# A new order for the first unit of a fused attention and feed-forward kernel, with some scalings and low parts moved to GpSimd

## The chip, the cores and the metric

One core of a Trainium2 chip runs the whole kernel. The metric is device microseconds of one execution; the shown times are of three executions. TensorE multiplies matrices, VectorE and ScalarE work on tiles element by element (ScalarE also does the exponentials), GpSimd is the fourth compute engine, and SyncE issues loads. In the profile they are PE, DVE, ACT, POOL and SP.

## What is computed

Attention with 4 batches, 8 heads, 576 positions and head size 64, in two patterns: four heads see a plain band of 32 keys, four see every fourth key of the last 128. Then two feed-forward blocks on the 2304 tokens:

```python
attn = softmax(where(mask, q @ k.T / 8, -1e9)) @ v      # band of 32, or 32 keys in steps of 4
h = maximum(maximum(x @ w1, x @ w2), x @ w3)            # 512 -> 768
x = h @ w_out
h = x @ w_in                                            # 512 -> 2048
g = (a0 + a1*h + a2*h**2 + a3*h**3) / (1 + |b0|*|h| + |b1|*h**2 + 1e-6)
out = g @ w_out2
```

Weights arrive as float64; attention inputs and result are float32.

## The kernel before

**Two-part numbers.** Matrix products of the feed-forward blocks are made of three TensorE passes: a value is split into a high part (rounded by a ScalarE copy into the matmul's type) and a low part (the rest, by a subtraction), and high x high, high x low and low x high are summed (`mm3`). A float64 weight tile of 128x512 goes through five steps: `L` (load of the words, SyncE's queue, `cv_load` L521), `up` (`cv_up` L543, ScalarE), `bits` (`cv_bits` L552, VectorE, two operations), `hi` (`cv_hi` L560, ScalarE) and `lo` (`cv_lo` L573, VectorE: the subtraction of L579). `up` writes a buffer "cvt" that `lo` is the last to read; there are three of them (`CVT`, L156). The first unit converts 24 tiles so, 18 of the three input matrices and 6 of the output matrix.

**Units.** Tokens of the first block go in five units; the first has 384 tokens, two attention parts (0 and 1) of 192 positions. While the first unit's matmuls run, parts 2 and 3 of the attention are made for the next unit. Each part has a plain (p) and a dilated (d) half. All of the first unit is one list of words, `START` (L36), written out by hand: each word is issued in the list's order, and each engine takes its own instructions in that order (`manual_schedule`, L728). The words of a part: `S` scores and mask on TensorE (L302), `MX` maxima (VectorE), `D` subtraction (VectorE), `E` exponentials (ScalarE), `SM` sums, `SB` scaling by one over the sum (L406: two small VectorE operations, then a multiplication of the whole tile on VectorE, or with `act` one ScalarE copy per head and block), `X` transposes on TensorE (L417), `XC` copies of these out of PSUM, `V` the product with the values, `VH` and `VL` its high and low parts. `W:n` puts 4n multiplications of a dummy tile ahead of the next bank. Of the first block: `P:i` is the product with weight tile i (12 matmuls), `M:i` the maximum taken over the three matrices, `HH` and `HL` the parts of the result, `Y` the output columns (18 matmuls each), `YS` their copy out. A word in lower case with a digit is a load (`kp0`, `qd1`, `v0`). For c=3 the dilated scores have fewer keys than the tile's width, so `S3:d` also issues a fill of the rest on GpSimd:

```python
            if W < WD and not plain:
                nc.gpsimd.memset(sb[:, :, W:WD], 0.0)     # L350
```

The dilated tiles of parts 2 and 3 share one buffer. Behind the first unit come four more, then the second block, whose schedule is not touched.

Of the kernel before, what the change touches and what calls it, by code (L numbers as in the profile page):

```python
# [7 lines left out]
F32 = mybir.dt.float32  # L8
F32R = mybir.dt.float32r
AF = mybir.ActivationFunctionType  # L10
ALU = mybir.AluOpType
# [22 lines left out]


START = """  # L36
mk mkB T kp0 qp0 qd0 W:8 S0:p kd0 MX0:p kd1 E0:p W:4 S0:d,mm SM0:p MX0:d qd1 D0:d E0:d SB0:p S1:d
X0:p,1 L SM0:d MX1:d X0:p,0,pv up kp1 qp1 S1:p,mm SB0:d XC0:p,1 bits E1:d L up MX1:p D1:p
XC0:p,0 v0 X0:d,1,sc X0:d,0,pv XC0:d,0 XC0:d,1 W:2 V0:p,mm SB1:d V0:d,sc X1:d,1 bits qd2 v1 E1:p
X1:d,0,mm SM1:p hi lo L L qp2 SB1:p S2:d,pv XC1:d,1 X1:p,0 XC1:d,0 VH0:p VH0:d hi XC1:p,0 L  # L40
X1:p,1,mm VL0:p V1:d,mm L MX2:d up XC1:p,1 VL0:d V1:p,mm VH1:d bits VH1:p VL1:d S2:p VL1:p lo up hi
P:0 up MX2:p L P:1 E2:d lo bits P:2 hi M:0 k1 up bits L SB2:d M:1 lo bits P:3 L hi E2:p up M:2 lo L
bits L hi lo M:3 up HH:0 P:4 X2:d,1,mm bits hi qp3 up hi lo L X2:d,0,pv L SB2:p,act bits S3:p P:5 up
L M:4 lo XC2:d,1 L MX3:p P:6 X2:p,1 qd3 XC2:d,0 S3:d,pv L bits M:5 hi X2:p,0,mm up lo bits P:7 HL:0
up hi M:6 HH:1 lo bits MX3:d up hi XC2:p,0 lo hi L up bits lo M:7 E3:p P:8 P:9 hi bits lo M:8 up
P:12 L L hi bits E3:d lo hi SM3:d M:9 up lo HL:1 HH:2 up XC2:p,1 bits M:12 hi v2 bits L up hi
SB3:d,act P:10 lo M:10 up P:13 L bits P:11 M:13 L SM3:p P:14 V2:p,sc hi HL:2 V2:d,sc SB3:p,act M:11
lo X3:p,0 up lo bits L M:14 hi bits up X3:d,0,pv bits HH:4 XC3:p,0 L X3:d,1,mm hi X3:p,1,pv lo v3
HH:3 lo P:16 HL:4 hi XC3:d,1 lo up P:15 HL:3 up P:17 bits XC3:d,0 VH2:d M:15 bits up XC3:p,1 hi
VH2:p M:16 bits lo V3:p hi M:17 V3:d,tp lo VH3:p hi VH3:d lo HH:5 HL:5 Y:2 VL2:d VL3:d Y:0 YS:0 YS:2  # L50
Y:3 VL3:p YS:3 Y:1 VL2:p YS:1
"""

UNITS = {3: """
# [49 lines left out]
def kernel(  # L104
# [16 lines left out]
    nc = tc.nc  # L121
# [19 lines left out]
    M = CH // 4  # L141
# [147 lines left out]
    def attn_pieces(c):  # L289
# [116 lines left out]
        def SB(g, engine="dve"):  # L406
            sv, Q, W, U, sm = grp[g][:5]
            nc.vector.tensor_scalar_add(sm, sm, 1.0e-9)
            nc.vector.reciprocal(sm, sm)
            if engine == "dve":  # L410
                nc.vector.tensor_tensor(out=sv, in0=sv, in1=sm.to_broadcast([Q, U, W]),
                                        op=ALU.mult)
                return
            for n in range(U):
                nc.scalar.activation(out=sv[:, n], in_=sv[:, n], func=AF.Copy, scale=sm[:, n])
# [58 lines left out]
        def VL(g):  # L474
# [3 lines left out]
            if done_v[c] == 2 and c > 2:  # L478
                load_v(c + 1)

        return {"S": SC, "MX": MX, "D": DF, "E": E, "SM": SM, "SB": SB, "X": X, "XC": XC,
                "V": V, "VH": VH, "VL": VL}

    at_fn = {}

    def do(word):

        op, _, arg = word.partition(":")
        name, c = op.rstrip("0123456789"), int(op.lstrip("ABCDEFGHIJKLMNOPQRSTUVWXYZ"))
        if c not in at_fn:  # L490
            at_fn[c] = attn_pieces(c)
        at_fn[c][name](*[x if x.isalpha() else int(x) for x in arg.split(",")])
# [77 lines left out]
        cv[i][3] = slot  # L570
        nc.scalar.activation(out=slot[:, 0:512], in_=cv[i][2], func=AF.Copy)

    def cv_lo(i):  # L573
        kind, f, j = conv_seq[i]
        _, _, t, slot = cv.pop(i)
        if kind == "w2":
            nc.gpsimd.dma_start(out=w2d[f], in_=t)
        else:
            nc.vector.tensor_sub(slot[:, 512:1024], t, slot[:, 0:512].bitcast(F32))  # L579

    cv_at = {"load": 0, "up": 0, "bits": 0, "hi": 0, "lo": 0}
    cv_steps = (("hi", cv_hi, "bits"), ("lo", cv_lo, "bits"), ("up", cv_up, "load"),
                ("bits", cv_bits, "up"), ("load", cv_load, None))

    def w2_words(k):

        i = n_w1 + k
        cv_up(i)
        cv_bits(i)
        cv_lo(i)  # L590
        if k + RAW2 < 2 * F2:
            cv_load(i + RAW2)
# [11 lines left out]
    def m1_mm(u, f, j, cols=None):  # L604
        if (u, f, j) not in m1:
            m1[u, f, j] = bank("mm", "mm")[:, 0:SZ1[u]]
        cols = cols or slice(0, SZ1[u])
        x1h, x1l = x1[u]
        w = w1s[f, j]
        mm3(m1[u, f, j][:, cols], [(w[:, 128 * c:128 * c + 128], w[:, 512 + 128 * c:640 + 128 * c],  # L610
                                    x1h[:, c, cols], x1l[:, c, cols]) for c in range(KC)])

    def m1_max(u, f, j):
        o = m1[u, f, j]
        if j == 0:
            m1[u, f] = com.tile([128, T1], F32, tag="m", bufs=MB, name="m")[:, 0:SZ1[u]]
            nc.scalar.activation(out=m1[u, f], in_=o, func=AF.Copy)
        else:
            nc.vector.tensor_tensor(out=m1[u, f], in0=o, in1=m1[u, f], op=ALU.max)  # L619
# [75 lines left out]
    with ExitStack():  # L695
# [4 lines left out]
        mk = const.tile([128, 512], F32, name="mk")  # L700
# [17 lines left out]
        script = START.split()  # L718
        steps = {n: (fn, after) for n, fn, after in cv_steps}

        def cv_step(name):
            fn, after = steps[name]
            assert cv_at[name] < (cv_at[after] if after else n_w1)
            assert name != "lo" or cv_at["lo"] < cv_at["hi"]
            fn(cv_at[name])
            cv_at[name] += 1

        with tc.manual_schedule():  # L728
            for word in script:
                op, _, arg = word.partition(":")  # L730
                if op == "L":
                    cv_step("load")
                elif op in loads:
                    loads[op]()
                elif op == "W":
                    idle[0] = int(arg)
                elif op == "H":
                    m1_mm(0, 0, int(arg), slice(0, CH))
                elif op == "P":
                    f, j = divmod(int(arg), 3)  # L740
                    m1_mm(0, f, j, slice(CH if (0, f, j) in m1 else 0, 2 * CH))
                elif op == "M":
                    m1_max(0, *divmod(int(arg), 3))
                elif op in ("HH", "HL", "Y", "YS"):
                    {"HH": m1_hh, "HL": m1_hl, "Y": m1_y, "YS": m1_ys}[op](0, int(arg))
                elif op in steps:
                    cv_step(op)
                else:
                    do(word)

# [19 lines left out]
        for u in range(1, NU):  # L770
            last = u == NU - 1
            pieces = attn(u + 1) if not last else iter(())
            if last:
# [9 lines left out]
                with tc.high_priority(offset=-LATE_W2):  # L783
                    for _ in range(W2A):
                        load_w2(w2a)
                    for tag in ("x1h", "x1l"):
                        t = xa.tile([128, NP * T1], F32R, tag=tag, name="w2x")
                        load_w2(xa, t[:, 0:1024])
                        load_w2(xa, t[:, 1024:2048])
            slot = 0  # L790
# [132 lines left out]
        for g in range(NSL + 4):  # L923
            t, c = divmod(g, F2)
# [154 lines left out]
```

## Time and profile before

| | us |
|---|---|
| median of three executions (776.42 to 777.43) | 777.36 |
| the profiled execution | 777.2 |
| its span, first to last instruction | 775.4 |
| TensorE busy in the span | 767.7 |
| VectorE busy | 585.7 |
| ScalarE busy | 452.4 |
| GpSimd busy | 59.1 |

The profiled execution takes 1.8 us more than its span: what lies around the first and last instruction. It stands 0.16 us below the median. Busy times overlap, so they don't add up. GpSimd's busy time is nearly all the issuing of transfers. The first unit's list runs from the start of the span to about 86 us, where the last of its output columns is copied out.

### The profile page before, as it was taken

How to read it: one execution, taken by the hardware profiler on the slowest of the kernel's cores; microseconds unless marked ns; L12 is line 12 of the kernel's file. 1: busy time of each engine (PE TensorE's matmuls, PEld its weight loads, DVE VectorE, ACT ScalarE, POOL GpSimd, SP SyncE). 2: the span in 40 equal slices, each digit the busy share in tenths (PEclk: the TensorE clock that was granted, in tenths of full speed). 3: DMA queues.
4: the chain of work that ended last, by engine and by line, in shares of the span. 5: the costliest groups of instructions: out<-in, count | busy, mean ns of one | idle time of the engine just before them, and what ended most of it. 6: DMA issues, size and time to landing. Idle time of an engine off the chain costs nothing.

```text
span 775.4 us, 12062 instructions
## 1 busy us (share of the span) xinstructions
PE 767.7 (99%) x4656; PEld 661.1 (85%) x4656; DVE 585.7 (76%) x997; ACT 452.4 (58%) x841; POOL 59.1 (8%) x114
## 2 busy tenths in 40 slices
PE   8999999999999999999999999999999999999997
PEld 7999999988888888888888888888888888888996
DVE  5999477567635663465499998889888998888983
ACT  4997243333332333243597878677776768676872
POOL 0000222213121101000000001000000001000010
PEclk9999999999999999999999999999999999999999
DMA  9981577657556556632400011000110001000010
GB/s 342 401 347 49 173 227 240 192 167 232 194 168 182 163 184 219 204 109 88 143 0 1 1 55 55 1 1 3 66 42 1 1 27 55 1 0 1 1 55 27
DMA packets 28490, 85.67 MB, mean 110 GB/s; under 512 B 3664, under 2 KB 5456, under 8 KB 28432
## 3 DMA queue, kind: packets, MB, share of 16 engines
q1 hardware_dynamic: 19344, 52.17, 21.3%
q0 software_dynamic: 8800, 32.51, 11.4%
q8 instruction: 36, 0.59, 0.3%
q10 hardware_dynamic: 288, 0.22, 0.1%
q14 instruction: 22, 0.18, 0.1%
HBM read 67.06 MB, written 17.83 MB: 109 GB/s over the span
## 4 chain that ended last, share of the span: by engine, by line
PE 98%; ACT 1%; DVE 1%; issue 0%; ACTq 0%
PE mm L597 13%; PE mm L598 13%; PE mm L599 13%; PE h L597 8%; PE h L599 8%; PE h L598 8%; PE acc L909 8%; PE acc L911 8%; PE acc L910 8%; PE sc L341 3%; PE tpp L424 2%; PE pv L455 1%; PE pv L447 1%; PE sc L207 0%; ACT keys L397 0%; DVE mx L369 0%
## 5 line engine op out<-in xcount | busy, mean ns | idle before, releaser
L597 PE MATMUL mm<-x1h,w1s 128*128 128x512 f32 (+1 forms) x360 | 134.5, 374 | 0.0
L599 PE MATMUL mm<-x1h,w1s 128*128 128x512 f32 (+1 forms) x360 | 132.4, 368 | 0.0
L598 PE MATMUL mm<-x1l,w1s 128*128 128x512 f32 (+1 forms) x360 | 132.4, 368 | 0.0
L599 PE MATMUL h<-x2h,w2s 128*128 128x512 f32 (+1 forms) x280 | 103.0, 368 | 0.0
L598 PE MATMUL h<-x2l,w2s 128*128 128x512 f32 (+1 forms) x280 | 103.0, 368 | 0.0
L597 PE MATMUL h<-x2h,w2s 128*128 128x512 f32 (+1 forms) x280 | 103.0, 368 | 0.0
L909 PE MATMUL acc<-w2s,gh 128*128 128x512 f32 x252 | 98.1, 389 | 0.0
L910 PE MATMUL acc<-w2s,gh 128*128 128x512 f32 x252 | 98.1, 389 | 0.0
L911 PE MATMUL acc<-w2s,gl 128*128 128x512 f32 x252 | 96.2, 389 | 0.0
L857 ACT ACTIVATE q<-h 128x512 f32<-128x512 f32 x72 | 43.1, 598 | 85.4 <-PE h L599 84.1
L597 PEld LDWEIGHTS mm<-x1h,w1s 128*128 128x128 f32 x360 | 67.6, 188 | 9.1
L599 PEld LDWEIGHTS mm<-x1h,w1s 128*128 128x128 f32 x360 | 67.6, 188 | 8.6
L864 DVE SCALAR_TENSOR_TENSOR q<-q,cs,ab 128x512 f32<-128x512 f32 x72 | 54.0, 750 | 27.5 <-ACT ab L858 26.6
L598 PEld LDWEIGHTS mm<-x1l,w1s 128*128 128x128 f32 x360 | 67.7, 188 | 8.1
L619 DVE TENSOR_TENSOR m<-mm,m 128x512 f32<-128x512 f32 (+1 forms) x60 | 38.0, 633 | 35.3 <-PE mm L599 30.4
L598 PEld LDWEIGHTS h<-x2l,w2s 128*128 128x128 f32 x280 | 52.8, 189 | 8.9
L597 PEld LDWEIGHTS h<-x2h,w2s 128*128 128x128 f32 x280 | 52.7, 188 | 8.8
L599 PEld LDWEIGHTS h<-x2h,w2s 128*128 128x128 f32 x280 | 52.8, 188 | 8.8
L859 ACT ACTIVATE p<-h,cs 128x512 f32<-128x512 f32 x72 | 56.5, 785 | 0.4 <-DVE gl L894 0.4
L911 PEld LDWEIGHTS acc<-w2s,gl 128*128 128x128 f32 x252 | 47.3, 188 | 9.9
L909 PEld LDWEIGHTS acc<-w2s,gh 128*128 128x128 f32 x252 | 47.3, 188 | 9.7
L910 PEld LDWEIGHTS acc<-w2s,gh 128*128 128x128 f32 x252 | 47.3, 188 | 9.7
(121 smaller groups left out, 1494.0 us busy)
## 6 DMA issues: line engine op xcount, KB each, us to landing
w1r<-in_w_dram SPq DMA_DIRECT2D x18, 512.0 KB, 9.1
raw<-in_w_in_dram SPq DMA_DIRECT2D x16, 512.0 KB, 4.3
w2d<-cvt POOLq DMA_DIRECT2D x32, 256.0 KB, 4.7
raw<-in_w_out_dram SPq DMA_DIRECT2D x16, 512.0 KB, 4.1
w2s<-w2d SPq DMA_DIRECT2D x28, 256.0 KB, 2.9
vd<-in_vd_dram POOLq DMA_DIRECT2D x8, 512.0 KB, 5.6
x2l<-x2d SPq DMA_DIRECT2D x4, 1024.0 KB, 7.0
out_dram<-ob POOLq DMA_DIRECT2D x16, 256.0 KB, 2.8
```

The source lines that it names most:

```text
L341: nc.tensor.matmul(o[h], lhsT=l, rhs=r, start=not pem, stop=not pem or n % G == G - 1)
L424: nc.tensor.transpose(tp[:, i, :], sv[:, G * j + i, :], ident[:Q, :Q])
L597: nc.tensor.matmul(o, lhsT=lh, rhs=rh, start=(i == 0), stop=False)
L598: nc.tensor.matmul(o, lhsT=lh, rhs=rl, start=False, stop=False)
L599: pe_at[0] = nc.tensor.matmul(o, lhsT=ll, rhs=rh, start=False, stop=(i == n - 1))
L619: nc.vector.tensor_tensor(out=m1[u, f], in0=o, in1=m1[u, f], op=ALU.max)
L857: nc.scalar.activation(out=s["q"], in_=s["h"], func=AF.Square)
L859: nc.scalar.activation(out=s["p"], in_=s["h"], func=AF.Identity, scale=cs[:, 3:4], bias=cs[:, 2:3])
L864: nc.vector.scalar_tensor_tensor(out=s["q"], in0=s["q"], scalar=cs[:, 5:6], in1=s["ab"], op0=ALU.mult, op1=ALU.add)
L909: nc.tensor.matmul(o, lhsT=gh, rhs=w[:, 0:512], start=(c == 0), stop=False)
L910: nc.tensor.matmul(o, lhsT=gh, rhs=w[:, 512:1024], start=False, stop=False)
L911: nc.tensor.matmul(o, lhsT=gl, rhs=w[:, 0:512], start=False, stop=(c == F2 - 1))
```

## The change

`START` is replaced by another order of the same words (the three loads `qp0`, `kd0`, `kp0` now come in this order at the front; four `W` words hold 13 groups of dummy multiplications where three held 14; `S3:d` comes ahead of the transposes `X2:d`). `SB` takes `pool`, which puts the multiplication of the tile on GpSimd while the two small operations stay on VectorE: parts 0, 2 and 3, both halves. Before, SB0:p, SB0:d and SB2:d multiplied on VectorE, SB2:p, SB3:d and SB3:p on ScalarE; part 1 stays on VectorE. `lo:pool` puts the subtraction of a low part on GpSimd: the weights 0, 1 and 3 to 7. `XC0:p,0` moves from ScalarE to VectorE. The line numbers stay as they are.

```diff
--- before.py
+++ after.py
@@ -34,21 +34,21 @@
 
 
 START = """
-mk mkB T kp0 qp0 qd0 W:8 S0:p kd0 MX0:p kd1 E0:p W:4 S0:d,mm SM0:p MX0:d qd1 D0:d E0:d SB0:p S1:d
-X0:p,1 L SM0:d MX1:d X0:p,0,pv up kp1 qp1 S1:p,mm SB0:d XC0:p,1 bits E1:d L up MX1:p D1:p
-XC0:p,0 v0 X0:d,1,sc X0:d,0,pv XC0:d,0 XC0:d,1 W:2 V0:p,mm SB1:d V0:d,sc X1:d,1 bits qd2 v1 E1:p
-X1:d,0,mm SM1:p hi lo L L qp2 SB1:p S2:d,pv XC1:d,1 X1:p,0 XC1:d,0 VH0:p VH0:d hi XC1:p,0 L
-X1:p,1,mm VL0:p V1:d,mm L MX2:d up XC1:p,1 VL0:d V1:p,mm VH1:d bits VH1:p VL1:d S2:p VL1:p lo up hi
-P:0 up MX2:p L P:1 E2:d lo bits P:2 hi M:0 k1 up bits L SB2:d M:1 lo bits P:3 L hi E2:p up M:2 lo L
-bits L hi lo M:3 up HH:0 P:4 X2:d,1,mm bits hi qp3 up hi lo L X2:d,0,pv L SB2:p,act bits S3:p P:5 up
-L M:4 lo XC2:d,1 L MX3:p P:6 X2:p,1 qd3 XC2:d,0 S3:d,pv L bits M:5 hi X2:p,0,mm up lo bits P:7 HL:0
-up hi M:6 HH:1 lo bits MX3:d up hi XC2:p,0 lo hi L up bits lo M:7 E3:p P:8 P:9 hi bits lo M:8 up
-P:12 L L hi bits E3:d lo hi SM3:d M:9 up lo HL:1 HH:2 up XC2:p,1 bits M:12 hi v2 bits L up hi
-SB3:d,act P:10 lo M:10 up P:13 L bits P:11 M:13 L SM3:p P:14 V2:p,sc hi HL:2 V2:d,sc SB3:p,act M:11
-lo X3:p,0 up lo bits L M:14 hi bits up X3:d,0,pv bits HH:4 XC3:p,0 L X3:d,1,mm hi X3:p,1,pv lo v3
-HH:3 lo P:16 HL:4 hi XC3:d,1 lo up P:15 HL:3 up P:17 bits XC3:d,0 VH2:d M:15 bits up XC3:p,1 hi
-VH2:p M:16 bits lo V3:p hi M:17 V3:d,tp lo VH3:p hi VH3:d lo HH:5 HL:5 Y:2 VL2:d VL3:d Y:0 YS:0 YS:2
-Y:3 VL3:p YS:3 Y:1 VL2:p YS:1
+mk mkB T qp0 kd0 kp0 qd0 kd1 qd1 W:8 S0:p qp1 kp1 L MX0:p S0:d,mm W:3 S1:d,pv MX0:d D0:d W:1 S1:p,mm
+E0:p E0:d SM0:p SB0:p,pool X0:p,1 qd2 MX1:d SM0:d SB0:d,pool MX1:p X0:p,0,mm D1:p XC0:p,0,dve E1:d
+W:1 X0:d,0,sc v0 E1:p XC0:p,1 L v1 up qp2 X0:d,1,mm S2:d,pv XC0:d,0 SB1:d SM1:p L XC0:d,1 X1:d,0
+V0:p,mm SB1:p V0:d,sc XC1:d,0 L VH0:p X1:p,0,mm X1:p,1 up XC1:p,0 X1:d,1,sc XC1:p,1 XC1:d,1 VH0:d
+bits VL0:p qp3 hi V1:p,mm bits VL0:d lo:pool VH1:p V1:d,tp S2:p VL1:p VH1:d up VL1:d L L hi k1 up
+MX2:d MX2:p E2:d qd3 bits bits lo:pool hi P:0 SB2:d,pool L lo L P:1 up L bits M:0 S3:p,pv up bits hi
+MX3:p lo:pool hi lo:pool L P:2 L E2:p L P:3 up hi M:1 M:2 up S3:d,mm M:3 bits X2:d,1,sc bits X2:d,0
+hi HH:0 lo:pool up P:4 L MX3:d lo:pool SB2:p,pool E3:d up bits hi HL:0 hi lo:pool XC2:d,0 SM3:d M:4
+bits L P:5 P:6 X2:p,1 hi lo up M:5 X2:p,0,sc lo bits up up L L bits hi E3:p hi M:6 P:7 P:9 lo
+XC2:p,0 SB3:d,pool L v2 bits SM3:p XC2:p,1 lo M:7 P:10 hi up up HH:1 lo bits hi L M:9 SB3:p,pool
+P:11 up bits M:10 lo bits hi P:8 M:11 P:12 L up L hi HH:3 XC2:d,1 lo M:8 lo V2:d,sc bits up V2:p,sc
+bits M:12 hi lo X3:p,1,pv VH2:d up up X3:d,0,pv X3:d,1,mm hi X3:p,0 L HL:1 bits lo bits hi XC3:d,1
+up P:15 HH:2 L hi lo bits lo L P:13 up XC3:p,0 bits M:15 XC3:d,0 up HL:2 M:13 VH2:p hi bits hi L hi
+lo v3 P:14 M:14 P:16 lo M:16 up P:17 bits lo M:17 HH:4 XC3:p,1 V3:p,tp hi HH:5 V3:d VH3:p HL:3 VH3:d
+HL:4 HL:5 lo Y:2 VL3:p Y:1 YS:2 Y:3 YS:1 VL2:d VL2:p VL3:d Y:0 YS:3 YS:0
 """
 
 UNITS = {3: """
@@ -407,9 +407,9 @@
             sv, Q, W, U, sm = grp[g][:5]
             nc.vector.tensor_scalar_add(sm, sm, 1.0e-9)
             nc.vector.reciprocal(sm, sm)
-            if engine == "dve":
-                nc.vector.tensor_tensor(out=sv, in0=sv, in1=sm.to_broadcast([Q, U, W]),
-                                        op=ALU.mult)
+            if engine != "act":
+                engine = nc.vector if engine == "dve" else nc.gpsimd
+                engine.tensor_tensor(out=sv, in0=sv, in1=sm.to_broadcast([Q, U, W]), op=ALU.mult)
                 return
             for n in range(U):
                 nc.scalar.activation(out=sv[:, n], in_=sv[:, n], func=AF.Copy, scale=sm[:, n])
@@ -570,13 +570,13 @@
         cv[i][3] = slot
         nc.scalar.activation(out=slot[:, 0:512], in_=cv[i][2], func=AF.Copy)
 
-    def cv_lo(i):
+    def cv_lo(i, engine=nc.vector):
         kind, f, j = conv_seq[i]
         _, _, t, slot = cv.pop(i)
         if kind == "w2":
             nc.gpsimd.dma_start(out=w2d[f], in_=t)
         else:
-            nc.vector.tensor_sub(slot[:, 512:1024], t, slot[:, 0:512].bitcast(F32))
+            engine.tensor_sub(slot[:, 512:1024], t, slot[:, 0:512].bitcast(F32))
 
     cv_at = {"load": 0, "up": 0, "bits": 0, "hi": 0, "lo": 0}
     cv_steps = (("hi", cv_hi, "bits"), ("lo", cv_lo, "bits"), ("up", cv_up, "load"),
@@ -718,11 +718,11 @@
         script = START.split()
         steps = {n: (fn, after) for n, fn, after in cv_steps}
 
-        def cv_step(name):
+        def cv_step(name, *engine):
             fn, after = steps[name]
             assert cv_at[name] < (cv_at[after] if after else n_w1)
             assert name != "lo" or cv_at["lo"] < cv_at["hi"]
-            fn(cv_at[name])
+            fn(cv_at[name], *engine)
             cv_at[name] += 1
 
         with tc.manual_schedule():
@@ -744,7 +744,7 @@
                 elif op in ("HH", "HL", "Y", "YS"):
                     {"HH": m1_hh, "HL": m1_hl, "Y": m1_y, "YS": m1_ys}[op](0, int(arg))
                 elif op in steps:
-                    cv_step(op)
+                    cv_step(op, *[nc.gpsimd] * (arg == "pool"))
                 else:
                     do(word)
```

## Rows read from the trace of the kernel before

**Rows 1.** The page's first part: each engine's busy time over the span.

```profile
PE 767.7 (99%) x4656; PEld 661.1 (85%) x4656; DVE 585.7 (76%) x997; ACT 452.4 (58%) x841; POOL 59.1 (8%) x114
```

**Rows 2.** TensorE's waits, whole span: engine, line, waited for, us, times, longest.

```profile
PE pv L447 <- ACT pt L435: 0.8, 1, 0.8
PE tpp L424 <- DVE sb L411: 0.7, 1, 0.7
PE tpp L424 <- ACT keys L397: 0.6, 1, 0.6
PE tpp L424 <- ACT w1s L571: 0.3, 1, 0.3
PE sc L341 <- DMA qTd<-in_qd_dram: 0.2, 1, 0.2
```

**Rows 3.** TensorE in order of time: start us, us, engine, line, operation.

```profile
4.39 0.69 PE L325 MATMUL sc<-mk 128*128 128x288 bf16 x2
5.01 1.88 PE L341 MATMUL sc<-keys,qTp 64*64 64x96 f32 x24
6.82 1.07 PE L207 MATMUL sc<-warm 128*128 128x128 bf16 x16
7.72 0.33 PE L325 MATMUL sc<-mk 96*96 96x192 bf16 x2
...
12.19 0.86 PE L424 MATMUL tpp<-mk,sb 128*96 128x128 f32 x6 [0.68 <-DVE sb L411]
...
15.73 0.61 PE L207 MATMUL pv<-warm 128*128 128x128 bf16 x8
...
25.84 0.44 PE L597 MATMUL mm<-x1h,w1s 128*128 128x384 f32 x1
...
75.90 0.44 PE L598 MATMUL mm<-hhl,wo1s 128*128 128x384 f32 x1
```

**Rows 4.** Windows: us; busy us (count) of PE, PEld, DVE, ACT, POOL; clock, DMA, GB/s.

```profile
10.00:25.00 15.00, 12.57 (x216) 11.17 (x218) 14.55 (x39) 11.41 (x36) 0.00 (x0) 1.00 1.03 404
25.00:75.00 50.00, 50.00 (x435) 48.78 (x431) 48.94 (x104) 46.22 (x129) 0.31 (x1) 1.00 0.69 265
```

**Rows 5.** VectorE in order of time, columns as in rows 3.

```profile
11.38 0.76 DVE L411 TENSOR_TENSOR sb<-sb,sm 128x576 f32<-128x576 f32 x1
...
31.43 0.68 DVE L579 TENSOR_TENSOR w1s<-cvt,w1s 128x512 fp32r<-128x512 f32 x1
32.03 0.42 DVE L555 TENSOR_SCALAR cvt<-cvt 128x512 int32<-128x512 int32 x1
...
33.09 0.55 DVE L619 TENSOR_TENSOR m<-mm,m 128x384 f32<-128x384 f32 x1
...
75.29 0.55 DVE L629 TENSOR_TENSOR hhl<-m,hhl 128x384 fp32r<-128x384 f32 x1
```

**Rows 6.** First, second, fourth load (us to landing); issue of the third.

```profile
keys<-in_kp_dram SPq DMA_DIRECT2D x1, 192.0 KB, 2.7
...
qTp<-in_qf_dram SPq DMA_DIRECT2D x1, 192.0 KB, 3.1
...
keys<-in_kd_dram SPq DMA_DIRECT2D x1, 192.0 KB, 5.7
...
1.67 0.42 SPq L262 DMA_DIRECT2D qTd<-in_qd_dram  x1
```

**Rows 7.** ScalarE's scalings by shape, first unit.

```profile
L415 ACT ACTIVATE sb<-sb,sm 128x96 f32<-128x96 f32 x12 | 3.4, 362 | 0.9 <-DVE sm L409 0.9
...
L415 ACT ACTIVATE sb<-sb,sm 96x48 f32<-96x48 f32 x8 | 1.9, 326 | 0.0
```

**Rows 8.** GpSimd's fills by shape, and the second one in order of time.

```profile
L350 POOL MEMSET sb<- 96x256 f32 x4 | 1.2, 308 | 42.6 <-PE tpp L424 42.3 <-POOLq L1062 0.3
L1062 POOL MEMSET const-uint8-127<- 128x1 uint8 x1 | 0.1, 113 | 0.0
...
37.31 0.31 POOL L350 MEMSET sb<- 96x256 f32 x1 [36.25 <-PE tpp L424]
```

## The prediction

> **What bounds it now.** The page first: TensorE is busy 99% of the span, GpSimd 8% [rows 1]. So the time can change only where TensorE stands idle, multiplies the dummy tile, or would come to wait. The list of TensorE's waits [rows 2] gives five after the first scores, 0.8 + 0.7 + 0.6 + 0.3 + 0.2 = 2.6 us. TensorE's order of time [rows 3] places them: they lie between 4.39 us, when the first score matmul starts, and 25.84 us, when the first weight matmul (word P:0) starts. In the same stretch the dummy matmuls of the second and third "W" take 0.9 us (6.82 to 7.72, 16 of them, so 0.056 us each) and 0.6 us. Idle and dummy together are 4.1 us, real work 25.84 - 4.39 - 4.1 = 17.35 us. That 4.1 us is all a new order of the first unit can win: from P:0 on TensorE is full (50.00 of 50 us [rows 4]).
>
> The windows [rows 4] show the second limit: VectorE is busy 14.55 of 15 us before 25 us and 48.94 of 50 after. In its order of time [rows 5] the last low half (HL:5) starts at 75.29 and ends at 75.84 us; the matmul of the first output column that reads it starts at 75.90 [rows 3]. VectorE has thus no slack: had P:0 started earlier alone, TensorE would have waited for HL:5. From P:0 to that matmul TensorE needs 75.90 - 25.84 = 50.1 us without a hole. After that both have room (VectorE needs nothing for unit 1's matmuls but the four subtractions behind HL:5), and all later stages are left as they are.
>
> **The sum, step 1: start of P:0.** The same 18 attention words stand ahead of P:0 as before, in another order, so its real work stays 17.35 us and I count the holes. Plain keys kp0 are now the third load and not the first. Issues are 0.45 us apart; the first two loads took 2.7 and 3.1 us, the fourth (also 192 KB) 5.7 us [rows 6]. The third, issued at 1.67 [rows 6], lands between 1.67 + 3.1 = 4.8 and 1.67 + 5.7 = 7.4; scores started at 5.01 [rows 3], so the delay is 0 to 2.4 us, and I take 0.8, near the low end since its size is that of the second load. S0:d and S1:d need the same first four and six loads as before and don't move. Holes then: 0.8 (kp0), 0.7 (W:3, standing for the sixth load), 0.4 (two W:1), 0.2 (X0:d for GpSimd's scaling of SB0:d), 0.4 (V1:p for its last XC copy). That is 2.5 against 4.1: P:0 at 24.2 us, **1.6 us earlier** (0 to 2.4 by the load's bounds). VectorE's scaling of SB0:p was the wait of 0.7 us; with S1:p now ahead of X0:p TensorE comes about 1.3 us later, so GpSimd's doing it is covered as long as that takes under about 2 us. Its cover gone, every microsecond over goes into P:0.
>
> **Step 2: what VectorE saves.** Back to back, a low part holds it 0.60 us (31.43 to 32.03) and a "bits" pair 1.06 (32.03 to 33.09) [rows 5]. Gone before HL:5: 7 low parts and one that moves behind HL:5, 4.8 us; three scalings, SB0:p (0.76 [rows 5], spaced 0.68) and SB0:d and SB2:d scaled from it by width, 1.9 us. Added: one copy XC0:p,0, 0.5 us. HL:5 would end at 75.8 - 4.8 - 1.9 + 0.5 = 69.6 us; the new order makes VectorE wait some 1.5 us more early on (first maxima later, scores of part 1 later), so 71.1. ScalarE loses SB2:p, SB3:p (3.4 us for both) and SB3:d (1.9) [rows 7]; I cost that at nothing, since no wait of TensorE but the early 0.8 us [rows 2] ends at a ScalarE copy.
>
> **Step 3: GpSimd's price.** The trace has no arithmetic on GpSimd. Bounds from its fills [rows 8]: 0.308 us for 256 elements, 0.113 for one, hence 0.77 ns per element and 0.11 fixed. 512 elements in one pass: 0.5 us. Two reads in a row: 0.9. Two reads and a write, each by itself: 1.3. I take 1.1, between the last two, as nothing shows two accesses overlapping; 96x384 is then 0.85, 128x576 1.2, 96x640 1.35. Ten GpSimd operations behind P:0 (six low parts, four scalings) are 11.2 us.
>
> **Step 4: GpSimd's own queue.** The fill of line 350 for S3:d waits for X2:d to have left the buffer: before, GpSimd stood 36.25 us and filled at 37.31 [rows 8], with nothing behind it. Now S3:d stands ahead of X2:d, and the sixth low part, later the seventh, queue behind that fill. X2:d ends near 36.1 us in the new order, so the sixth low part ends near 37.6 instead of 34.4. P:5, which needs it, comes at 38.2: covered by 0.6. But "cvt" has three buffers, so the ninth "up" on ScalarE waits for this low part, and behind it E3:d and the "bits" that VectorE runs next. VectorE waits some 1.8 us: HL:5 at **72.9**, while TensorE wants it at 24.2 + 50.1 = 74.3. Slack 1.4 us.
>
> **Step 5: do the two engines hinder each other?** No row decides. Lower end 0: side by side. Upper end: each GpSimd operation stops VectorE as soon as VectorE reaches one that reads two tiles of SBUF (bits, low parts, HL); these fill some three quarters of its time behind P:0, since those with one operand in PSUM (maxima, M, VL) are few there. Going through the order: the scalings ahead of P:0 and the first low part have PSUM work beside them, no cost. Behind P:0: second low part 0.35, SB2:d 1.35 (a low part of VectorE is next), 1.1 and 0.2, two at 0 as VectorE waits anyway, SB2:p 1.2, 0.35, SB3:d 0.85, SB3:p 1.2: **6.6 us**. With GpSimd at 0.9 for 512 this is 5.1, at 1.3 8.2.
>
> I take the upper end: GpSimd's 11.2 us are put beside a VectorE 98% busy [rows 4], and the slack is 1.4 us. It takes 1.4 us of stops to cost anything and 3.0 to use up the gain, a quarter of 11.2.
>
> The page "SBUF — State Buffer" of the Trainium skill (section "Who interferes with whom") has it that a VectorE instruction with two SBUF inputs contends with a GpSimd instruction that reads SBUF, the second to come being blocked whole; no run here shows it yet. By it the change ends slower, by its opposite faster; the Trainium skill's "GPSIMD Engine Reference" (section "Elementwise — side-by-side cycle accounting") gives 4497 ns for 2048 elements, by which 512 would be an estimated 1.1 us.
>
> **Sum.** HL:5 at 72.9 + 6.6 = 79.5, against 74.3: TensorE waits 5.2 us in the output columns, or as much spread over earlier P words. Less 1.6: **+3.6 us**. The profiled execution took 777.2 us (span 775.4 and 1.8 around it), the median is 777.36; so 781.0.
>
> **Rivals.**
> 1. *Side by side* (the other sign): the engines don't hinder each other. For it: no row shows a VectorE operation stretched. Against: nothing here lets GpSimd read. VectorE ends at 72.9, TensorE stays full, -1.6 us: 775.8; with kp0 landing at once -2.4, 775.0. It decides as long as the stops stay under 1.4 us. Chance 0.37; 0.24 of it over the 0.2% (1.55 us, about what a measurement of this kernel can tell from none), 0.13 within, since -1.6 stands right at it.
> 2. *Stops, but few*: GpSimd finds gaps, VectorE loses 1.5 to 4 us. The result lies between -1.6 and +1.0: 777. Chance 0.12, mostly within.
> 3. *GpSimd late at the start*: its first multiplication takes much over the 2 us of cover, or the first keys land at 7.4. Each microsecond moves P:0; at 3 us of delay 1.4 us slower: 778.8. Chance 0.05.
> 4. *It doesn't do what it says*: the order is written out by hand and TensorE's and VectorE's sequence in [rows 3, 5] is that of the list, so this gets 0.01.
>
> **The numbers.** Forecast 0.45, of it 0.03 within 0.2%. Faster 0.24 + 0.05 from the second rival = 0.29; within 0.13 + 0.07 + 0.03 = 0.23; slower 0.48. Both signs hold much: the likeliest case alone runs from +1.7 (GpSimd 0.9: HL:5 at 72.5 + 5.1 = 77.6, 3.3 late) to +5.4 (1.3: 73.1 + 8.2 = 81.3, 7.0 late), 779.1 to 782.8. The range reaches from the side-by-side case with most of its gain, 775.2, to that upper end with 0.4 of key delay on top, 783.2.
>
> **What would show it.** Right: P:0 near 24.2 us; GpSimd's subtraction 128x512 near 1.1 us and VectorE's bits or low parts lengthened, or gaps ahead of them, while GpSimd runs; TensorE waits for VectorE that were not there, in P words or output columns, 5 us in all; GpSimd idle ahead of the fill of S3:d. Wrong: VectorE's operations unchanged at 0.68 to 0.69 us beside GpSimd's, TensorE full from P:0 to unit 1; then the gain is what P:0 gained. If P:0 starts later than 25 us, step 1 failed.

## The result, and the profile after

The changed kernel takes 782.88 us, the median of six executions (781.17 to 785.07); the kernel before, run beside it, 776.46 (776.12 to 777.43). The ratio is **1.0079**, 95% interval 1.0068 to 1.0090: 6.4 us slower, where 781.0 had been forecast and the range ended at 783.2. The profiled execution is the shortest of the six: 781.17 us, span 779.4. Against the 775.4 of before that is 4.0 us; the other 2.4 us of the medians are taken up below.

The page's first part, as [rows 1]: GpSimd works 17 us more, VectorE no less than before although seven low parts and three scalings are gone from its first unit.

```profile
PE 767.9 (99%) x4652; PEld 660.1 (85%) x4652; DVE 589.8 (76%) x988; ACT 447.9 (57%) x820; POOL 76.0 (10%) x127
```

TensorE's waits of the changed kernel, columns as in [rows 2]:

```profile
PE mm L597 <- ACT sb L397: 1.8, 1, 1.8
PE sc L325 <- DVE m L619: 1.8, 2, 1.3
PE mm L597 <- ACT m L617: 1.1, 2, 0.7
...
PE sc L341 <- DMA keys<-in_kp_dram: 0.6, 1, 0.6
PE sc L341 <- DMA qTd<-in_qd_dram: 0.4, 1, 0.4
PE tpp L424 <- POOL sb L412: 0.3, 1, 0.3
PE mm L599 <- POOL w1s L579: 0.2, 1, 0.2
```

The last four are the start and one low part. The first three, 4.7 us, did not exist before: for a scores tile that ScalarE reads late, for maxima that VectorE takes late (M:1 and M:2, L619), and for the copy by which ScalarE begins each group of three maxima (L617). TensorE in order of time, as [rows 3], says where they are:

```profile
4.32 0.41 PE L325 MATMUL sc<-mk 128*128 128x288 bf16 x2
5.33 1.21 PE L341 MATMUL sc<-keys,qTp 64*64 64x96 f32 x24 [0.60 <-DMA keys<-in_kp_dram]
...
23.00 0.44 PE L597 MATMUL mm<-x1h,w1s 128*128 128x384 f32 x1
...
35.09 0.24 PE L325 MATMUL sc<-mk 96*96 96x192 bf16 x1 [1.34 <-DVE m L619]
35.75 0.24 PE L325 MATMUL sc<-mk 96*96 96x192 bf16 x1 [0.42 <-DVE m L619]
...
42.00 0.45 PE L597 MATMUL mm<-x1h,w1s 128*128 128x384 f32 x1 [1.84 <-ACT sb L397]
...
51.97 0.44 PE L597 MATMUL mm<-x1h,w1s 128*128 128x384 f32 x1 [0.70 <-ACT m L617]
```

P:0 starts at 23.00 us, 2.84 earlier than before; then come the waits, between 31 and 57 us. The window of [rows 4] shows the loss as a whole: TensorE is idle 4.93 of 50 us where it was full, beside a VectorE just as busy as before (48.94).

```profile
25.00:75.00 50.00, 45.07 (x334) 42.20 (x333) 48.94 (x88) 38.43 (x102) 12.35 (x10) 1.00 0.70 269
```

The last output column of the first unit is copied out at 89.90 us, at 85.94 before: +3.96, the whole difference of the two spans. From P:0 to that copy it is 66.9 us against 60.1, so 6.8 are lost there and 2.8 won ahead of it.

**Why VectorE is as busy.** Its groups by line and shape up to 85 us: first the kernel before, then the changed one (count, busy us, mean ns).

```profile
L557 DVE SCALAR_TENSOR_TENSOR cvt<-w1r,cvt 128x512 int32<-128x512 int32 x18 | 12.5, 692 | 0.6
...
L555 DVE TENSOR_SCALAR cvt<-cvt 128x512 int32<-128x512 int32 x24 | 10.0, 417 | 0.0
```

```profile
L557 DVE SCALAR_TENSOR_TENSOR cvt<-w1r,cvt 128x512 int32<-128x512 int32 x18 | 16.5, 919 | 0.6
L555 DVE TENSOR_SCALAR cvt<-cvt 128x512 int32<-128x512 int32 x24 | 11.6, 483 | 0.0
...
L372 DVE TENSOR_SCALAR mx<-mx 96x8 f32<-96x8 f32 x3 | 4.1, 1376 | 0.1
```

The same instructions on the same tiles take 4.0 and 1.6 us more in all, and the scaling of the dilated maxima, 96x8 numbers, takes 4.1 us for three. A page of groups hides which of them were hit; the order of time shows it. VectorE, then GpSimd, of the changed kernel:

```profile
28.88 1.63 DVE L557 SCALAR_TENSOR_TENSOR cvt<-w1r,cvt 128x512 int32<-128x512 int32 x1
30.43 1.51 DVE L555 TENSOR_SCALAR cvt<-cvt 128x512 int32<-128x512 int32 x1
31.98 1.66 DVE L557 SCALAR_TENSOR_TENSOR cvt<-w1r,cvt 128x512 int32<-128x512 int32 x1
...
38.38 2.60 DVE L372 TENSOR_SCALAR mx<-mx 96x8 f32<-96x8 f32 x1
...
77.68 1.49 DVE L629 TENSOR_TENSOR hhl<-m,hhl 128x384 fp32r<-128x384 f32 x3
```

```profile
10.93 1.15 POOL L412 TENSOR_TENSOR sb<-sb,sm 128x576 f32<-128x576 f32 x1 [9.88 <-DVE sm L409]
...
21.37 1.28 POOL L579 TENSOR_TENSOR w1s<-cvt,w1s 128x512 fp32r<-128x512 f32 x1 [7.41 <-ACT w1s L571]
...
28.12 1.84 POOL L412 TENSOR_TENSOR sb<-sb,sm 96x640 f32<-96x640 f32 x1 [3.56 <-DVE sm L409]
29.93 3.17 POOL L579 TENSOR_TENSOR w1s<-cvt,w1s 128x512 fp32r<-128x512 f32 x2
38.17 0.31 POOL L350 MEMSET sb<- 96x256 f32 x1 [5.08 <-PE tpp L424]
38.44 2.53 POOL L579 TENSOR_TENSOR w1s<-cvt,w1s 128x512 fp32r<-128x512 f32 x2
```

From 28.1 to 33.1 us GpSimd works without a break, and three VectorE operations of 0.69, 0.42 and 0.69 us elsewhere take 1.63, 1.51 and 1.66. So VectorE comes to M:1 and M:2 3.0 us later, and TensorE, whose scores of S3:d want their banks, waits 1.34 + 0.42. From 38.4 to 41.0 the 96x8 operation lasts exactly as long as two low parts on GpSimd. GpSimd pays too: the two low parts from 29.93 took 3.17 us, the next two 2.53. The page "SBUF — State Buffer" of the Trainium skill (section "Who interferes with whom") says that a VectorE instruction with two SBUF inputs contends with a GpSimd instruction that reads SBUF, and that the second to come is blocked whole; the two rows of L557, 1.63 and 1.66 us for 0.69, agree with it.

ScalarE in order of time shows how this reaches P:5 at 42.00:

```profile
39.76 0.67 ACT L547 ACTIVATE cvt<-w1r 128x512 f32<-128x512 f32 x1 [1.86 <-POOL w1s L579]
41.08 1.62 ACT L397 ACTIVATE sb<-sc,mx 96x48 f32<-96x48 f32 x8 [0.65 <-DVE sm L408]
```

GpSimd stood 5.08 us ahead of the fill of S3:d (38.17 above), so the sixth low part came late and ScalarE's "up" waited 1.86 us for its buffer. E3:d, which frees the bank that P:5 writes, stands behind that "up" and needs the 96x8 scaling, done at 40.98. Both were late.

VectorE's total up to the end of HL:5, before and after (us; VectorE's busy us and count; clock, DMA, GB/s):

```profile
0.00:75.84 75.84, 66.71 (x153) 1.00 0.76 291
0.00:79.17 79.17, 70.17 (x143) 1.00 0.74 279
```

It stands idle for 9.1 us in the one and 9.0 in the other: with ten operations fewer it ends 3.3 us later, and all of that is operations that take longer.

### The profile page after: what moved, and what is told of

The parts are those of the page before. It is cut to its first block, busy times and chain, and to the rows that moved or that the text cites. A ratio compares the mean times of both kernels' runs of the same rounds, so it can differ in the third digit from the quotient of the medians.

```text
span 779.4 us, 12060 instructions
## 1 busy us (share of the span) xinstructions
PE 767.9 (99%) x4652; PEld 660.1 (85%) x4652; DVE 589.8 (76%) x988; ACT 447.9 (57%) x820; POOL 76.0 (10%) x127
## 4 chain that ended last, share of the span: by engine, by line
PE 92%; DMA 5%; DVE 1%; SPq 0%; issue 0%; ACT 0%
PE mm L597 12%; PE mm L598 12%; PE mm L599 12%; PE h L597 8%; PE h L599 8%; PE h L598 8%; PE acc L909 8%; PE acc L911 8%; PE acc L910 8%; PE sc L341 3%; PE tpp L424 2%; PE pv L455 1%; DMA w1r<-in_w_dram 1%; DMA kTp<-in_kp_dram 1%; PE pv L447 1%; DMA vp<-in_vp_dram 1%
## 5 line engine op out<-in xcount | busy, mean ns | idle before, releaser
L599 PE MATMUL mm<-x1h,w1s 128*128 128x512 f32 (+1 forms) x360 | 132.6, 368 | 0.2 <-POOL w1s L579 0.2
L599 PE MATMUL h<-x2h,w2s 128*128 128x512 f32 (+1 forms) x280 | 103.0, 368 | 0.0
L597 PEld LDWEIGHTS mm<-x1h,w1s 128*128 128x128 f32 x360 | 67.6, 188 | 13.2 <-ACT sb L397 2.2
L599 PEld LDWEIGHTS mm<-x1h,w1s 128*128 128x128 f32 x360 | 67.6, 188 | 9.1 <-POOL w1s L579 0.5
L619 DVE TENSOR_TENSOR m<-mm,m 128x512 f32<-128x512 f32 (+1 forms) x60 | 38.0, 633 | 35.4 <-PE mm L599 30.6
L599 PEld LDWEIGHTS h<-x2h,w2s 128*128 128x128 f32 x280 | 52.7, 188 | 8.8
```

The source lines that it names most:

```text
L597: nc.tensor.matmul(o, lhsT=lh, rhs=rh, start=(i == 0), stop=False)
L599: pe_at[0] = nc.tensor.matmul(o, lhsT=ll, rhs=rh, start=False, stop=(i == n - 1))
```

## The experiments

**Theory A** is the prediction's: the new order alone is a gain or nothing, and the loss comes from VectorE and GpSimd stopping each other, and from the fill in GpSimd's queue. **Theory B**: the new order itself loses the time, whoever does the work. **Theory C** of the expectations: nothing is stopped, GpSimd only takes longer and whoever needs its results waits. Where times of kernels are compared, each is by its ratio to the kernel before on the same chip. Diffs are against the changed kernel unless another is named; of `START` they show the words alone.

**1. Only the order.** All scalings and low parts back on the engines of before; the copy XC0:p,0 stays on VectorE.

```diff
-SB0:p,pool SB0:d,pool SB2:d,pool SB2:p,pool SB3:d,pool SB3:p,pool lo:pool (7 times)
+SB0:p SB0:d SB2:d SB2:p,act SB3:d,act SB3:p,act lo (7 times)
```

> The new order with every scaling and low part on the engine that had it before (GpSimd computes nothing). Theory A (GpSimd and VectorE take turns at SBUF, which stretched VectorE's operations by 9.2 us in the changed kernel: bits 4.1 + 1.6, the small scaling of the maxima 3.6): VectorE ends HL:5 at 79.1 - 9.2 + 4.2 (seven low parts at 0.60) + 1.9 (three scalings) = 76.0 us, about where it ended before, so the time is that of the kernel before within 0.2%: 776 to 778 us. Theory B (the new order itself is what costs, by what it puts ahead of what): still 781 us or more. Theory C (no turn-taking; GpSimd only takes longer for its operations and those who need them wait): the gain of the earlier P:0 shows whole, 773.5 to 775 us.

784.01 us, ratio 1.0095 (1.0079 to 1.0112). Theory A's number fell: with nothing on GpSimd and VectorE's operations at their old length (692 and 414 ns), the new order costs as much. Theory C's number (775 at most) falls too. TensorE's order of time has waits again, P:5's at 42.39 and those for L617 in the same places, and a new one at 28.32:

```profile
28.32 0.44 PE L599 MATMUL mm<-x1h,w1s 128*128 128x384 f32 x1 [1.95 <-DVE w1s L579]
42.39 0.44 PE L597 MATMUL mm<-x1h,w1s 128*128 128x384 f32 x1 [1.96 <-ACT sb L397]
52.65 0.45 PE L597 MATMUL mm<-x1h,w1s 128*128 128x384 f32 x1 [1.01 <-ACT m L617]
58.58 0.44 PE L597 MATMUL mm<-x1h,w1s 128*128 128x384 f32 x1 [1.47 <-ACT m L617]
```

The first is the low part of weight 1, which the list puts behind two "bits" pairs and which is now VectorE's own. For the second, ScalarE's order of time:

```profile
39.88 1.71 ACT L415 ACTIVATE sb<-sb,sm 128x96 f32<-128x96 f32 x6 [0.91 <-DVE sm L409]
41.49 1.59 ACT L397 ACTIVATE sb<-sc,mx 96x48 f32<-96x48 f32 x8
```

The scaling SB2:p, back on ScalarE, stands ahead of E3:d. VectorE's low parts in turn wait 4.2 us for ScalarE's high parts (L571), where they waited for nothing before:

```profile
L579 DVE TENSOR_TENSOR w1s<-cvt,w1s 128x512 fp32r<-128x512 f32 x18 | 12.2, 684 | 4.2 <-ACT w1s L571 4.2
```

This wait is gone in experiment 2, where GpSimd does the scalings. The new order is laid out for a ScalarE without these copies and a VectorE without these low parts; with them it is worse than the old one.

**2 and 3. Half of the offload each.** First the scalings on GpSimd and the low parts on VectorE, then the reverse.

```diff
-lo:pool (7 times)
+lo (7 times)
```

> The changed kernel with its seven low parts back on VectorE; GpSimd does the six scalings alone. Theory A: the scalings' share of the stretches (SB2:d 0.9, SB2:p 0.8, SB3:d 0.5, SB3:p 0.8, SB0:p 0.3, together 3.3 us) against 1.9 us saved on VectorE: HL:5 near 77.4 us, time 777 to 779.5 us. Theory B: 781 or more. Theory C: 773.5 to 775.5.

```diff
-SB0:p,pool SB0:d,pool SB2:d,pool SB2:p,pool SB3:d,pool SB3:p,pool
+SB0:p SB0:d SB2:d SB2:p,act SB3:d,act SB3:p,act
```

> The changed kernel with its six scalings back on VectorE and ScalarE; GpSimd does the seven low parts alone. Theory A: the low parts' share of the stretches, some 5.9 us, against 4.2 us saved, and the queue behind the fill of S3:d still holds two of them: 778 to 781 us, slower than with the scalings alone. Theory B: 781 or more. Theory C: 774 to 777 (the fill's queue alone).

780.93 us (1.0057, 1.0036 to 1.0078) and 785.05 (1.0109, 1.0092 to 1.0126). Both come out above what theory A expected. With the scalings alone L557 is at 813 ns, and the low part of weight 1 again costs TensorE 1.93 us. With the low parts alone the 96x8 scaling is at 1269 ns, SB2:p is again ahead of E3:d, and the two together make P:5 wait 3.63 us. Both costs of the changed kernel are in the halves.

**4. Only what lies beside PSUM work.** The scalings of part 0 and the first low part stay on GpSimd.

```diff
-SB2:d,pool SB2:p,pool SB3:d,pool SB3:p,pool lo:pool (the last 6)
+SB2:d SB2:p,act SB3:d,act SB3:p,act lo (the last 6)
```

> The new order, GpSimd keeping only what VectorE's PSUM work stands beside: the scalings SB0:p and SB0:d and the low part of weight 0; all else on the engine that had it before. Theory A: 0.3 us of stretch against 1.75 us saved: VectorE ends HL:5 near 74.5 us, 1.3 before the kernel before: 774.5 to 776.5 us, the best of these four. Theory B: 781 or more. Theory C: no better than the order alone.

782.35 us, 1.0078 (1.0059 to 1.0096): a miss like the first, with the same waits (1.7, 1.9, 2.5 us). Hardly anything is stretched (L557 692, L555 414 ns; three 96x8 scalings 0.3 us in all), so GpSimd's help is nearly free there, but the order behind P:0 decides.

**5 and 6. Extra work on GpSimd in the kernel before**: 14 unused operations after the words P:0 to P:13, multiplications that read SBUF for both inputs (here the same tile), or fills that only write. Against the kernel before (`gs` takes the place of a buffer not yet in use):

```diff
+        def dummy():
+            ...
+            d = nc.gpsimd.tensor_tensor(out=gs[0][:, 0:512], in0=gs[0][:, 512:1024],
+                                        in1=gs[0][:, 512:1024], op=ALU.mult)
+            tc.add_manual_dep(d.ins, pe_at[0].ins.name, PACE, reason="beside the words behind")
+        loads["G"] = dummy
-P:0 ... P:13
+P:0 G ... P:13 G
```

> The kernel before, with 14 extra GpSimd multiplications of a 128x512 tile nobody uses, one released by the end of each of the words P:0 to P:13; nothing waits for them. Theory A: each holds VectorE up by most of its 1.3 us where VectorE is at an operation on two SBUF tiles, and VectorE has no slack: 8 to 14 us slower, with bits, low parts and small scalings stretched. Theory C: no change, since nobody waits for them: 776 to 777.5 us. Theory B says nothing.

```diff
-            d = nc.gpsimd.tensor_tensor(out=gs[0][:, 0:512], in0=gs[0][:, 512:1024],
-                                        in1=gs[0][:, 512:1024], op=ALU.mult)
+            d = nc.gpsimd.memset(gs[0], 0.0)
```

> The same 14 places with a GpSimd fill of 128x1024 (0.9 us by the fills' price) in place of the multiplication: it writes SBUF and reads nothing. Theory A in the form that only reads take turns: no change, 776 to 777.5 us. Theory A in the form that any GpSimd access takes turns: 5 to 10 us slower. Theory C: no change.

The multiplications: 789.87 us, 1.0168 (1.0151 to 1.0185). Groups by line, VectorE and GpSimd:

```profile
L579 DVE TENSOR_TENSOR w1s<-cvt,w1s 128x512 fp32r<-128x512 f32 x18 | 14.7, 820 | 0.0
L557 DVE SCALAR_TENSOR_TENSOR cvt<-w1r,cvt 128x512 int32<-128x512 int32 x18 | 14.6, 814 | 0.6
L555 DVE TENSOR_SCALAR cvt<-cvt 128x512 int32<-128x512 int32 x24 | 13.3, 553 | 0.0
...
L721 POOL TENSOR_TENSOR gs<-gs 128x512 f32<-128x512 f32 x14 | 16.2, 1154 | 52.1 <-PE mm L599 52.1
```

Nothing waits for these multiplications and nothing else was touched but for one fill of their tile at the start, yet VectorE's three groups grow by 2.5 + 2.1 + 3.3 us, a small operation (L408, 96x8, 582 ns for 160) by 1.7, and the last copy of the unit moves from 85.94 to 95.39. This is theory A's mechanism by itself, and theory C, by which nothing would change, falls: some 9.6 us of VectorE's time for 16.2 of GpSimd's. The profile is 13.8 us longer; the 4.4 us behind the first unit, 2.4 of them a wait in the second block, stay unexplained.

The fills: 782.21 us, 1.0072 (1.0051 to 1.0094), 5.2 us slower and so at the lower end of what was expected if any access of GpSimd takes turns. The rows show less than that. The same groups:

```profile
L555 DVE TENSOR_SCALAR cvt<-cvt 128x512 int32<-128x512 int32 x24 | 12.7, 528 | 0.0
L557 DVE SCALAR_TENSOR_TENSOR cvt<-w1r,cvt 128x512 int32<-128x512 int32 x18 | 12.5, 692 | 0.6
L579 DVE TENSOR_TENSOR w1s<-cvt,w1s 128x512 fp32r<-128x512 f32 x18 | 12.2, 680 | 0.0
```

A GpSimd operation that only writes leaves VectorE's two-input operations as they are and stops only one-input ones, L555 and the small L372 (128x6, 384 ns for 172). So with two inputs it is the reads that collide. The profile is 3.3 us longer; the last copy moves 1.35 us, and a wait of 1.6 us far behind, in the second block, makes up most of the rest and stays unexplained. The medians' 5.2 us are thus not traced to the first unit.

**7. The fill of S3:d later**, with the sums of that part and not with its scores, so that no low part queues behind it.

```diff
-            if W < WD and not plain:
+            if W < WD and not plain and c != 3:
...
+            if c == 3 and g == "d":
+                nc.gpsimd.memset(grp[g][8][:, :, W:WD], 0.0)
```

> The changed kernel with the fill of S3:d issued with SM3:d and so behind the low parts in GpSimd's queue. If the queue behind the fill is a cost of its own: GpSimd's wait of 5.1 us ahead of the fill, ScalarE's wait of 1.9 us for a low part and TensorE's of 1.8 us at P:5 go, and the time falls by 1 to 2.5 us, to 780.5 to 782. If turn-taking alone decides, VectorE gets the same stretches elsewhere and the time stays within 0.1% of the changed kernel's 782.9.

781.21 us, 1.0069 (1.0042 to 1.0096): 0.8 us under the changed kernel by the ratios, but the intervals overlap, so the time does not tell them apart. In the profile ScalarE's wait for GpSimd's low part is gone, yet P:5's only goes from 1.84 to 1.46 us: the two low parts now come earlier and stop the "bits" pair that stands ahead of the scaling (lines moved down by two, so L557 and L559 are "bits"), and the scaling itself, unstopped at 0.17 us, is done only 1.0 us earlier behind P:0 than in the changed kernel (17.0 for 18.0):

```profile
39.30 1.50 DVE L557 TENSOR_SCALAR cvt<-cvt 128x512 int32<-128x512 int32 x1
40.83 1.67 DVE L559 SCALAR_TENSOR_TENSOR cvt<-w1r,cvt 128x512 int32<-128x512 int32 x1
```

With the fill out of the way the stop falls on other operations, and P:0 to the last copy gets 1.0 us shorter (65.9 for 66.9). TensorE's start in this profile, with the very same words, is another than above:

```profile
5.77 2.19 PE L341 MATMUL sc<-keys,qTp 64*64 64x96 f32 x24 [0.69 <-DMA keys<-in_kp_dram]
...
8.23 2.69 PE L341 MATMUL sc<-keys,qTd 128*96 128x48 f32 x16
...
26.22 0.44 PE L599 MATMUL mm<-x1h,w1s 128*128 128x384 f32 x1
```

The 24 and the 16 score matmuls take 2.19 and 2.69 us for 1.21 and 1.53, and P:0 starts at 26.22 (L599 here, moved by two lines) for 23.00.

**8. The dilated maxima scaled by ScalarE**, so that the 96x8 operation cannot be stopped.

```diff
+            if mode[g] != "B" and g == "d" and c < EARLY:
+                nc.scalar.activation(out=mx, in_=mx, func=AF.Copy, scale=-SCALE)
-            if mode[g] != "B":
+            elif mode[g] != "B":
                 nc.vector.tensor_scalar_mul(mx, mx, -SCALE)
```

> The changed kernel with the small scaling of the maxima (96x8, 3.6 us longer in three of them) done by ScalarE for the dilated halves. Theory A, whoever is stopped: the 3.6 us go, but part of them comes back at VectorE's next operation on SBUF: 1 to 3 us faster than the changed kernel, 780 to 782. Theory C: no change.

780.72 us, 1.0048 (1.0030 to 1.0066), which clears the changed kernel's interval: about 0.3%, 2.4 us, from three tiny operations. But the stop has moved rather than gone. The small operation that now stands beside the two low parts, 166 ns in the changed kernel, is held instead:

```profile
38.12 2.71 DVE L410 TENSOR_SCALAR sm<-sm 128x6 f32<-128x6 f32 x1
```

E3:d does not need it, and P:5's wait goes from 1.84 to 1.27 us. The "bits" L557 (L559 here) are still at 875 ns. How the rest of the 2.4 us comes about is not shown.

**9 and 10. The offload in the old order**: all six scalings and seven low parts, then only the three scalings that ScalarE had (SB2:p, SB3:d, SB3:p).

```diff
-(START of the change)
+(START of before, with SB0:p,pool SB0:d,pool SB2:d,pool SB2:p,pool SB3:d,pool SB3:p,pool lo:pool)
```

> The order of the kernel before with the same work moved to GpSimd (six scalings, low parts of weights 0, 1 and 3 to 7). Theory A (turn-taking at SBUF costs, whatever the order): VectorE saves 6.1 us and is stretched by 6 to 10, so HL:5 ends 0 to 4 us later than 75.8, and the early scalings on GpSimd delay P:0 by up to 1: 777.5 to 782 us. Theory B (the move pays, the new order is what costs): 773 to 776 us.

```diff
-(START of the change)
+(START of before, with SB2:p,pool SB3:d,pool SB3:p,pool)
```

> The order of the kernel before; only the three scalings that ScalarE did (SB2:p, SB3:d, SB3:p) go to GpSimd. Nothing is taken from VectorE, 5.3 us from ScalarE. Theory A: VectorE is stretched by 1.5 to 2.5 us and had no slack: 777.5 to 780 us. If ScalarE's 5.3 us were on the path (against the prediction, which costed them at nothing): 774 to 776.5.

779.38 us (1.0036, 1.0025 to 1.0048) and 778.98 (1.0029, 1.0017 to 1.0040). In the first L557 is at 829 ns, L555 at 531, L579 at 755, and HL:5 starts at 78.45 us, 3.2 later than before though VectorE has seven low parts and three scalings fewer. In the second ScalarE is 5.3 us of copies lighter and nothing gets faster: the relief buys nothing, the stops (L557 740, L579 726 ns) cost 1.6 us of VectorE. Theory B's second half, by which the offload alone would gain, falls. Its first half, that the new order loses, held in experiment 1 for the old engines.

**11. The new order up to P:0 only**, with `kp0` the first load again and the old words and engines behind. GpSimd keeps SB0:p, SB0:d and the low part of weight 0; that of weight 1 comes ahead of the two "bits" pairs.

```diff
-qp0 kd0 kp0 ... bits bits lo:pool hi P:0 (words of the change)
+kp0 qp0 kd0 ... lo bits bits hi P:0 (words of before)
```

> The words up to P:0 in the new order (plain keys loaded first again; GpSimd scales SB0:p and SB0:d and makes the low part of weight 0, beside which VectorE works out of PSUM), the words behind P:0 in the old order and on the old engines. P:0 should start at 22.5 to 23.5 us, 2.3 to 3.3 earlier. If VectorE is the second limit as the prediction has it, HL:5 ends at about 76 us as before and TensorE gives the 2.3 to 3.3 us back behind P:0: 776 to 778 us. If TensorE alone limits: 773.5 to 775.

776.40 us, 0.9996 (0.9987 to 1.0006): no change, although P:0 starts at 22.66, 3.2 us earlier. TensorE waits 1.1 us for two low parts of VectorE, and P:0 to the last copy is 62.1 us where it was 60.1. The last copy comes at 84.76, 1.2 earlier, and the median follows by 0.3. So 2.0 of the 3.2 us are lost again, over half of that in waits for a VectorE that is busy throughout: what VectorE as the second limit would do. The other 0.9 are not traced.

**12. The parts that helped, together**, in the new order: fill later (7), maxima on ScalarE (8), `kp0` first, all low parts on VectorE with weight 1's ahead of the two "bits" pairs; GpSimd keeps the six scalings.

```diff
-qp0 kd0 kp0 ... bits bits lo:pool hi P:0 ... lo:pool (the others)
+kp0 qp0 kd0 ... lo bits bits hi P:0 ... lo (the others)
```

> The changed kernel mended where the traces point: low parts on VectorE, that of weight 1 ahead of two bits pairs; plain keys loaded first; the fill with SM3:d; the dilated maxima scaled by ScalarE. GpSimd keeps the six scalings. Theory A: the wait at P:1 (1.9 us), at the keys and at P:5 go, VectorE keeps some 2.5 us of stretches: 776 to 779 us. Theory B: still over 780.

778.44 us, 1.0023 (1.0013 to 1.0033): 4.4 us under the change and still slower than before; L561, the L557 of above, is at 813 ns, and TensorE waits 1.4 us for a low part of VectorE's. No version beat the kernel before.

| kernel (one profile each) | words behind P:0 | on GpSimd | P:0 at | P:0 to last copy |
|---|---|---|---|---|
| before | old | none | 25.84 | 60.1 |
| 10 | old | 3 scalings | 25.44 | 62.0 |
| 9 | old | all | 25.91 | 63.2 |
| 11 | old, front new | SB0:p, SB0:d, 1 low part | 22.66 | 62.1 |
| 1 | new | none | 23.67 | 68.0 |
| 2 | new | 6 scalings | 23.26 | 65.6 |
| 3 | new | 7 low parts | 24.00 | 69.2 |
| 4 | new | SB0:p, SB0:d, 1 low part | 23.60 | 67.6 |
| changed | new | all | 23.00 | 66.9 |
| 7 | new | all, fill later | 26.22 | 65.9 |
| 8 | new | all, three maxima on ScalarE | 24.28 | 65.0 |
| 12 | new, mended | 6 scalings | 23.02 | 64.4 |

## Why the prediction came out right, and where it did not

The sign, the mechanism and the size of the profiled execution hold (+4.0 against +3.6). That the number fits so well is luck in part: errors in its terms went both ways.

- *What bounds the kernel*: right. TensorE from P:0 on, VectorE just behind it; experiment 11 starts P:0 3.2 us earlier and gains nothing that its interval can tell from none.
- *Step 1, P:0 at 24.2*: 23.00. The holes were sized well in sum: 0.60 (kp0) + 0.41 + 0.67 (W:3) + 0.23 and 0.39 (W:1) + 0.34 (SB0:d) = 2.64 us for 2.5. What failed is "its real work stays 17.35": 23.00 - 4.32 - 2.64 = 16.0. The first masks and scores took 0.41 and 1.21 us where [rows 3] have 0.69 and 1.88, which is 0.95 of the 1.3. That part is not the order's alone: the same 24 matmuls took 1.37 and 1.49 us with the old front in experiments 9 and 10, and 2.19 with the new one in 7 and 8.
- *Step 2*: VectorE's savings were right; the 1.5 us that it would wait more early on did not come (9.0 us idle for 9.1). ScalarE's relief at nothing was right only for the old order (10). The new order needs it (1, 4): it is its condition, not its gain.
- *Step 3, 1.1 us per low part*: 1.28 where nothing ran into it, 1.15 for 128x576 and 0.83 for 96x384 in the scalings. The upper bound from the fills, 1.3, was the better choice. The estimate by the Trainium skill's "GPSIMD Engine Reference" (section "Elementwise — side-by-side cycle accounting"), 1.1 us, is short by as much.
- *Step 4, the fill in GpSimd's queue*: right in place: GpSimd stood 5.08 us and ScalarE's "up" waited 1.86. But the 1.8 us were forecast as a wait of VectorE's, and VectorE did not wait there: the 96x8 scaling held it from 38.38 to 40.98. Step 5 had put the two low parts behind the fill at 0 "as VectorE waits anyway"; they cost the 2.4 us by which that operation is longer. That P:5 would be covered was wrong: E3:d, late, held its bank.
- *Step 5, 6.6 us of stops*: 4.0 + 1.6 + 3.6 (4.1 us for what takes 0.5) = 9.2. The mis-sized term: the prediction counted only operations that read two tiles of SBUF and left out the small one-input ones, which can wait for two whole low parts (2.60 us).
- *The sum*: HL:5 at 79.5, measured 77.68 + 1.49 = 79.2. The two waits of VectorE's that did not come, 1.5 + 1.8 = 3.3 us, offset the 2.6 us by which the stops were put too small; this is the luck. The lateness was paid in earlier P words, as the prediction allowed, 6.8 us for 5.2, since each late maximum or E3:d holds a bank. A gain of 2.8 for 1.6 made up for most of it, and 0.95 of that gain is the faster first matmuls of step 1.
- *What the prediction had not*: the new words behind P:0 cost some 8 us by themselves when the old engines do the work (1), so without the offload this order is no gain. The waits for L617 (1.1 us in the changed kernel) also stand in every other run with the new words but 3 (0.8 to 2.5 us) and in none with the old, so they may be the order's own. The two do not add up: offload alone is 1.0036, order alone 1.0095, both 1.0079. In the changed kernel the stops account for VectorE's lateness; that the order with the offload would gain without them is argued, not shown, as the work must lie on some engine.
- *The rivals*: side by side is ruled out by the stretched rows and by 5; few stops by 9.2 us of them; GpSimd late at the start by its 1.15 us for SB0:p and a wait of TensorE's of 0.34.
- *The 2.4 us between profiles and medians* are open. With the very same words up to it, P:0 starts at 23.00 us in the changed kernel's profile, at 24.28 in experiment 8's and at 26.22 in 7's, after a wait for the plain keys in all three (0.60, 0.86, 0.69). The wait alone does not decide it: behind waits of 0.90 to 1.44 us in 1 to 4 the 24 matmuls took 1.21. The seven kernels with `kp0` third spread by 2.4 to 5.1 us, 9 to 12 with `kp0` first by 0.5 to 1.5; but 5 and 6, also with `kp0` first, by 3.0 and 3.7. That the start explains the spread is argued, not shown.

## What to carry to other kernels

Before giving work of a full VectorE to GpSimd, list what VectorE runs at that moment: beside operations that read two tiles of SBUF, and beside the smallest one-input ones, it lost more than half a microsecond per microsecond of GpSimd's work here (9.6 for 16.2), so moving 0.6 us there for 1.3 us of GpSimd costs about what it saves or more. An order written for one division of the work was a loss under another (1): time order and division apart, each on the old other, before believing in either. And when an earlier start is to be won, ask first which engine stands right behind the bound.

## What the runs showed that was not expected

- An operation on 96x8 numbers, 168 ns by itself, took 2.60 us beside two low parts of GpSimd.
- GpSimd fills stretch VectorE's one-input operation on 128x512 (417 to 528 ns on average) and leave two-input ones exactly alone (692, 680).
- After a long wait TensorE ran at a lower clock: in experiment 5 it stood 2.81 us up to 57.01, and the granted clock reads 0.62 in the window with the end of this wait and 0.70 in the next, between its levels of 1.2 (0.5) and 2.4 GHz (1.0). From 59.06 on the 128x384 matmuls start 0.32 us apart, where they did 0.17 to 0.18 just before the wait. So a stop of VectorE can cost more than its own length. Windows of that profile, columns as in [rows 4]:

```profile
55.00:60.00 5.00, 2.40 (x6) 1.93 (x7) 4.93 (x9) 4.08 (x16) 0.84 (x1) 0.62 0.10 38
60.00:65.00 5.00, 5.00 (x22) 5.00 (x22) 4.93 (x10) 4.41 (x10) 1.26 (x2) 0.70 0.00 0
```

- In experiment 7's start the granted clock reads 1.00 all the same, in the window from 8 to 14 us, where the 16 score matmuls took about 1.75 times as long (2.69 us for 1.53). The column alone would not have shown it:

```profile
8.00:14.00 6.00, 6.00 (x43) 5.94 (x44) 2.92 (x10) 2.02 (x7) 0.91 (x1) 1.00 0.68 249
```
